# Retention and a bilinear FFN on one core: wide K^T V products with copied diagonal blocks in the opening, a later place for their totals, and the fifth group's outputs in one stretch

## The chip, the core and the metric

The kernel runs on one core of a Trainium2 chip. The engines of a core run their own queues of instructions, in order, and wait for each other by semaphores: TensorE (PE, matrix products into the PSUM banks, with PEld for the loads of its stationary operand), VectorE (DVE), ScalarE (ACT), GpSimd (POOL) and SyncE (SP, which issues most of the transfers). The metric is the device time of one execution in microseconds; lower is better. Three runs of the kernel before gave 324.79, 324.88 and 325.64 us, median 324.88.

## The reference

Inputs are `q`, `k`, `v` of shape (8 batches, 8 heads, 576 positions, 64), and three matrices of an FFN with 512 inputs, 1536 hidden units and 512 outputs. Everything is float32.

```python
scores = scale * np.matmul(q, k.transpose(0, 1, 3, 2))
Dmat = np.where(rel >= 0, gamma[:, None, None] ** rel[None, :, :], 0.0)
ret = scores * Dmat[None, :, :, :]
attn = np.matmul(ret, v)                  # (8, 8, 576, 64)
x = attn.transpose(0, 2, 1, 3).reshape(B * S, H * D)   # 4608 x 512
out = (x @ w_a) * (x @ w_b) @ w_out       # 4608 x 512
```

`rel` is the distance of a query from a key, and each head has its own `gamma` below 1. There is no softmax. So the attention can be computed in pieces: a block of queries needs its scores with the keys of its own block, and one 64 x 64 matrix per head, the sum of K^T V over all blocks before it (its "state"). The decay is put into the values (each row times a power of 1/gamma) and taken out again where the outputs are scaled.

## The kernel before

The 4608 tokens are worked on in FFN blocks of 512, 256, 256 and then seven of 512 tokens. A block makes, for each of twelve groups F of 128 hidden units, a product `pa` (x by w_a, line 869, or line 820 for the first two groups of the first block) and `pb` (x by w_b, line 884); ACT casts `pa` to `ha` (877), DVE multiplies `ha` by `pb` into `hT` (889), and twelve products `po` (831, 905) give 128 output rows, which ACT or DVE copies to `osb` and SP stores. The FFN is by far the larger part. The attention's work is put between its products.

The attention of the first 256 tokens of batches 0, 1 and 2 is done in six "steps", `STEPS` (line 165): step 0 is batch 0 with heads 0 to 3, step 1 batch 1 with heads 0 to 3, steps 2 and 3 the same batches with heads 4 to 7, steps 4 and 5 batch 2. A partition holds two neighbouring tokens, so partitions 0 to 63 are tokens 0 to 127 and partitions 64 to 127 the rest; `kp` is the token of a partition, `j` a pair of heads, `r` a head of the pair, and `half(i)` the lower or upper 64 partitions. Steps 0 to 3 make up the opening, before the first FFN product; steps 4 and 5 come later, between products of the first block. A step has these parts:

- `cast_step` (315) casts queries and keys to bfloat16 as `qkb`, `values_step` (318) multiplies the values by their decay into `vb`, each on an engine named in the call.
- `transpose_step` (329) turns `qkb` by four PE products for each of Q and K into a bank `tp`, and copies that to `qkT`.
- `score_step` (344) makes sixteen 64-column-wide score products into `sc`, which DVE masks into `sT` (360).
- `state_step` (366) makes K^T V by sixteen products of 64 x 64 (379): one tile `kvs[0]` for the first 128 tokens, one tile `kvs[1]` for the second 128. ACT copies the first into `state_after` (391), which the second half of the step's queries needs, and keeps both, as `own` (395) and `second` (396). `last_states` (403) does this for steps 1 and 3 together: 32 products, then two copies into `state_after` (412), one of `own` (414) and one of `second` (416).
- `open_step`, `step_states` (449) and `step_keys` (465) make the outputs, and `close_step` scales them on DVE into `xT` (486, 481), from which the FFN reads.
- `total_of(n)` (419), called later, adds `second` to `own` and casts the sum: the state after 256 tokens.

All other tokens are handled in "pairs" of 128-token pieces with all eight heads. Pairs 3, 4 and 5 are the second parts of batches 0, 1 and 2. For a pair, `keyed` makes K^T V, `matched` the scores and their mask, `open_outputs` (704) the products of the queries with the states (`from_states`, 668), and `close_outputs` (714) those of the scores with the values (`keys_into`, 681), into the same tile `o`; DVE then scales it in two operations (694). Between the two, `open_outputs` has ACT copy one column of `o` to a small tile named `fence` (711), so the instructions that follow and write that tile come after that copy.

The order on every engine is the order in which the program calls the parts. For the opening this is written out (lines 938 to 1015), with `warm` products (932) of a constant in between. From then on a list `todo` gives each piece of attention work a due count, in units of one 512-column product, and the work is issued at the next "edge" of the FFN's stream after that count: behind each `pb`, and behind every fourth product of the output stage. Small DVE and ACT pieces go into a list `later`, from which `pop` takes one at certain places, and `flush` all. Pair 5 (the "fifth group") is due as follows, in the third FFN block, where the edges of the output stage lie at 268, 272, 276, 280, 284 and 288:

```python
(252, stretch, (5, 4)), (274, open_alone, (5,)),
(278, close_outputs, (5,)), (336, stretch, (6, None)),
```

Of the kernel before, what the change touches and what calls it, by code (L numbers as in the profile page):

```python
# [10 lines left out]
FP32 = mybir.dt.float32  # L11
# [3 lines left out]
ALU = mybir.AluOpType  # L15
# [3 lines left out]
def kernel(  # L19
# [108 lines left out]
    def half(i):  # L128
        return slice(64 * i, 64 * i + 64)
# [99 lines left out]
    def pair_tables(step):  # L229
# [17 lines left out]
        else:  # L247
# [7 lines left out]
    second = sum_pool.tile([128, FIRST, HP, 64], FP32, tag="sums",  # L255
                           name="second")
# [58 lines left out]
    def cast_step(i, w, on):  # L315
        COPY[on](by_parity(natural[STEPS[i]][0][:, w]), given(i, w))  # L316
# [12 lines left out]
    def transpose_step(i, *ways):  # L329
        qkb, qkT = natural[STEPS[i]][0], transposed[STEPS[i]]  # L330
        tp = ps_ffn.tile([128, len(ways), 4, 128], BF16, tag="ab", name="tp")
        for to, (w, on) in enumerate(ways):
            for c in range(4):
                nc.tensor.transpose(tp[:, to, c, :],  # L334
                                    qkb[:, w, c * 128:c * 128 + 128],
                                    identity)
        for to, (w, on) in enumerate(ways):
            COPY[on](qkT[:, w], tp[:, to].rearrange("p c x -> p (c x)"))
# [5 lines left out]
    def score_step(i, place=None, tag="sc"):  # L344
        key = STEPS[i]
        sc = (place or ps_sc).tile([128, 2, 2, 2, 128], FP32, tag=tag,
                                   name="sc0")
        for j in (0, 1):
            for kp in (0, 1):
                for r, a in QUADS:  # L350
                    k0 = kp * 256 + j * 128 + a * 64
                    nc.tensor.matmul(  # L352
                        sc[half(a), r, j, kp],
                        transposed[key][half(r), 1, k0:k0 + 64],
                        queries(key, half(r), j, a),
                        start=(j == 0 and kp == 0), stop=True,
                        skip_group_check=True)
# [8 lines left out]
    def state_step(i, rest=None):  # L366
        state_copies(i, state_products(i, [
            ps_ffn.tile([128, 2, 64], FP32, tag="ab", name=f"kv0{a}")
            for a in (0, 1)], set(QUADS)), rest)

    def state_products(i, kvs, fresh):

        n, hh = STEPS[i]
        qkb, vb = natural[n, hh]
        for j in (0, 1):
            for kp in (0, 1):
                for a, r in QUADS:
                    e0 = kp * 256 + (2 * j + r) * 64
                    nc.tensor.matmul(kvs[a][half(r), j, :],
                                     qkb[half(a), 1, e0:e0 + 64],  # L380
                                     vb[half(a), e0:e0 + 64],
                                     start=(a, r) in fresh, stop=True,
                                     skip_group_check=True)
                    fresh.discard((a, r))
        return kvs

    def state_copies(i, kvs, rest=None):
        n, hh = STEPS[i]
        cs = slice(2 * hh, 2 * hh + 2)
        for r in (0, 1):  # L390
            nc.scalar.copy(state_after[half(r), n % 2, cs, half(r)],
                           kvs[0][half(r)])

        def keep():
            nc.scalar.copy(own_sums[n][:, cs], kvs[0])
            nc.scalar.copy(second[:, n, cs], kvs[1])

        if rest is None:
            keep()
        else:  # L400
            rest.append(keep)

    def last_states():

        own, later_half = kvs = [
            ps_ffn.tile([128, 2, 2, 64], FP32, tag="ab", name=f"kv1{a}")
            for a in (0, 1)]
        fresh = set(QUADS)
        for i in (1, 3):
            state_products(i, [kv[:, i // 2] for kv in kvs], fresh)  # L410
        for r in (0, 1):
            nc.scalar.copy(state_after[half(r), 1, :, half(r)],
                           own[half(r)].rearrange("p i j d -> p (i j) d"))
        nc.scalar.copy(own_sums[1],
                       own.rearrange("p i j d -> p (i j) d"))
        nc.scalar.copy(second[:, 1],
                       later_half.rearrange("p i j d -> p (i j) d"))

    def total_of(n):

        own = own_sums[n]
        if n < FIRST - 1:
            nc.gpsimd.tensor_tensor(own, own, second[:, n], op=ALU.add)
            nc.gpsimd.tensor_copy(own_states[n], own)
        else:
            nc.vector.tensor_tensor(own, own, second[:, n], op=ALU.add)
            nc.scalar.copy(own_states[n], own)
        sums_of[n, 0] = own

# [25 lines left out]
    def step_keys(i, fresh):  # L455

        n, hh = STEPS[i]
        vb = natural[n, hh][1]
        sT = scored.pop((n, hh))
        seen = set()  # L460
        for j in (0, 1):
            for kp in (0, 1):
                for a, r in QUADS:
                    e0 = kp * 256 + (2 * j + r) * 64
                    nc.tensor.matmul(  # L465
                        out_of(i, a)[half(r), 128 * j:128 * j + 128],
                        vb[half(a), e0:e0 + 64],
                        sT[half(a), r, j, kp],
                        start=(a in fresh and (a, r) not in seen), stop=True,
                        skip_group_check=True)  # L470
# [480 lines left out]
    warm(2, 512)  # L951
    score_step(0)
    warm(1, 512)
    state_step(0)
    transpose_step(2, (Q, "dve"))
    cast_step(2, K, "pool")
    cast_step(1, K, "pool")
    warm(2, 512)
# [14 lines left out]
    cast_step(3, K, "dve")  # L973
    score_step(1)
    cast_step(3, Q, "act")
    rest = []
    state_step(2, rest)
    warm(2, 512)
    transpose_step(3, (Q, "act"))
    transpose_step(3, (K, "dve"))  # L980
    rest.pop()()
    open_step(2)
    step_states(2, True)
    step_keys(2, {0})
# [2 lines left out]
    values_step(3, 0, nc.scalar)  # L987
    values_step(3, 1, pool_)
    load_w(*pieces[1], "b")
    score_step(3)  # L990
    close_step(2)
    last_states()
    for i, banks in ((1, ps_ffn), (3, ps_sc)):
        open_step(i, banks)
        step_keys(i, {0, 1})
    for i in (1, 3):
        step_states(i, False)
    for i in (1, 3):
# [4 lines left out]
    for c in (0, 1):  # L1003
        for F in range(WCOLS[0]):
            begin_with(F, c, 1)
    for piece in pieces[2:]:
        load_w(*piece)
    for i in (0, 1, 2):
# [56 lines left out]
    def third_turn():  # L1065
        for i in (4, 5):
# [83 lines left out]
```

## Time and profile before

| what | value |
|---|---|
| median of three runs | 324.88 us |
| profiled execution, its own time | 324.69 us |
| its span, first to last instruction | 322.9 us |
| PE busy | 313.5 us (97%), 3569 products recorded |
| DVE, ACT, POOL busy | 166.3, 130.8, 118.9 us |
| first product of the FFN (line 820) | 16.41 us from the start |
| first `pb` product (line 884) | 18.16 us |
| HBM | 37.75 MB read, 9.44 MB written |

A row of the timeline gives start and duration in us, the engine, the line, the operation, `out<-in` by the program's tile names, the form (for products `rows*columns` of the array first), and `xN` where N instructions in a row are shown as one; their duration is then that of all. In square brackets stands the idle time before and what ended it. A row of waits gives who waited for what: total, number of times, longest. A row by stretch gives its bounds, its length, and the busy time and count of PE, PEld, DVE, ACT and POOL, then the granted clock, the share of the transfer engines and GB/s. Durations of PE products include their way through the array, so one of 128 columns is shown with about 0.22 us though the next starts 0.06 us later.

### The profile page before, as it was taken

Reading aid. Unit: us, or ns where it says so; the run is one execution under the profiler, and the core shown is the slowest. Engines: PE = TensorE matmul, PEld = TensorE weight load, DVE = VectorE, ACT = ScalarE, POOL = GpSimd, SP = SyncE. Lnnn points to the kernel's source line nnn. Section 1 sums busy time; section 2 is a strip of 40 time slices with the busy share of each in tenths; the row PEclk is TensorE's granted clock in tenths of the full one; section 3 lists DMA queues with packets and bytes.
Section 4 is the critical chain, followed back from the end, with each engine's and each line's share of the span. In section 5 each row is a group of like instructions: output and inputs, shape, how many; then the busy total and the mean of one; then the engine's idle time right before and its main releaser. Section 6 shows DMA issues by size and latency. Waiting matters only on the chain.

```text
span 322.9 us, 8622 instructions
## 1 busy us (share of the span) xinstructions
PE 313.5 (97%) x3569; PEld 164.1 (51%) x3607; DVE 166.3 (51%) x296; ACT 130.8 (40%) x289; POOL 118.9 (37%) x159
## 2 busy tenths in 40 slices
PE   7899999999999999999999999999999999999996
PEld 3554457778444555454454545454445444444444
DVE  6745346667437664745374527461666256514411
ACT  7745653436335533523253324342433243313321
POOL 4990076574745365348174305550520000000000
DMA  8999999999999999899999169925840510031013
GB/s 216 253 204 207 263 227 197 193 176 207 197 213 234 201 193 229 214 223 262 209 208 194 67 146 199 215 67 146 202 78 28 135 37 2 2 97 32 1 25 107
DMA packets 146487, 50.90 MB, mean 158 GB/s; under 512 B 126736, under 2 KB 141968, under 8 KB 146448
## 3 DMA queue, kind: packets, MB, share of 16 engines
q1 hardware_dynamic: 140112, 45.37, 68.0%
q0 software_dynamic: 5808, 4.72, 9.3%
q8 instruction: 28, 0.46, 0.6%
q10 hardware_dynamic: 528, 0.26, 0.3%
q14 instruction: 11, 0.09, 0.1%
HBM read 37.75 MB, written 9.44 MB: 146 GB/s over the span
## 4 chain that ended last, share of the span: by engine, by line
PE 93%; DMA 2%; POOL 1%; issue 1%; SPq 1%; DVE 0%; POOLq 0%
PE pb L884 29%; PE pa L869 28%; PE po L905 27%; DMA vf<-in_v_dram 2%; PE po L831 2%; PE o L681 1%; PE sc L640 1%; PE o L668 1%; PE kv L573 1%; SPq L159 1%; POOL vb L326 1%; PE pa L820 1%; PE o L465 0%; PE tp L334 0%; POOL wb_sb L266 0%
## 5 line engine op out<-in xcount | busy, mean ns | idle before, releaser
L889 DVE TENSOR_TENSOR hT<-ha,pb 128x512 bf16<-128x512 bf16 (+1 forms) x120 | 75.9, 633 | 91.3 <-PE pb L884 83.3
L884 PE MATMUL pb<-xT,wb_sb 128*128 128x512 bf16 (+1 forms) x473 | 111.3, 358 | 0.5
L877 ACT CAST ha<-pa 128x512 bf16<-128x512 f32 (+1 forms) x120 | 64.8, 542 | 112.8 <-PE pa L869 108.2
L869 PE MATMUL pa<-xT,wa_sb 128*128 128x512 bf16 (+1 forms) x457 | 108.1, 357 | 1.1 <-issue 0.6
L905 PE MATMUL po<-wo_sb,hT 128*128 128x512 bf16 (+2 forms) x419 | 89.6, 367 | 1.6 <-issue 1.4
L884 PEld LDWEIGHTS <-wb_sb 128*128 128x128 bf16 x480 | 47.0, 98 | 46.2
L869 PEld LDWEIGHTS <-wa_sb 128*128 128x128 bf16 x472 | 45.4, 98 | 44.6
L905 PEld LDWEIGHTS <-hT 128*128 128x128 bf16 x432 | 40.4, 98 | 44.4
L519 POOL CAST qkb<-qf 64x1024 bf16<-64x1024 f32 x15 | 15.4, 1030 | 67.0 <-DMA qf<-in_q_dram 61.3
L530 POOL TENSOR_TENSOR vb<-vf,vs 128x1024 bf16<-128x1024 f32 (+1 forms) x17 | 28.8, 1699 | 12.7 <-DMA vf<-in_v_dram 7.5
L916 DVE COPY osb<-po 128x512 f32<-128x512 f32 (+2 forms) x16 | 10.4, 650 | 38.9 <-PE po L905 38.9
L914 ACT COPY osb<-po 128x512 f32<-128x512 f32 (+1 forms) x20 | 11.4, 572 | 46.2 <-PE po L905 43.3
L519 POOL CAST qkb<-kf 64x1024 bf16<-64x1024 f32 (+1 forms) x17 | 15.9, 933 | 14.8 <-DMA kf<-in_k_dram 14.4
L598 DVE TENSOR_TENSOR sums<-kv,sums 128x256 f32<-128x256 f32 x44 | 18.7, 424 | 2.8 <-PE kv L573 0.8
L649 DVE TENSOR_TENSOR sT<-sc,mask 128x512 bf16<-128x512 f32 x30 | 19.5, 682 | 0.0
L523 POOL CAST qkb<-kf 64x512 bf16<-64x512 f32 (+1 forms) x34 | 18.6, 575 | 1.0
L523 POOL CAST qkb<-qf 64x512 bf16<-64x512 f32 x30 | 17.6, 614 | 0.6
L694 DVE TENSOR_TENSOR xT<-o,qs 128x512 bf16<-128x512 f32 x24 | 15.5, 682 | 2.6 <-PE o L681 2.6
L601 ACT CAST states<-sums 64x512 bf16<-64x512 f32 x26 | 16.0, 617 | 0.3
L316 POOL CAST qkb<-kf 128x512 bf16<-128x512 f32 x4 | 2.4, 612 | 16.1 <-DMA kf<-in_k_dram 16.1
L360 DVE TENSOR_TENSOR sT<-sc,mask_s 128x1024 bf16<-128x1024 f32 x6 | 7.3, 1224 | 1.5 <-PE sc L352 1.3
L932 PE MATMUL w<-ones 128*128 128x512 bf16 x17 | 6.3, 483 | 1.5 <-DVE idxp_f L204 1.5
(96 smaller groups left out, 173.0 us busy)
## 6 DMA issues: line engine op xcount, KB each, us to landing
qf<-in_q_dram SPq DMA_DIRECT2D x32, 256.0 KB, 4.7
vf<-in_v_dram SPq DMA_DIRECT2D x32, 256.0 KB, 5.0
kf<-in_k_dram SPq DMA_DIRECT2D x31, 256.0 KB, 4.7
out_dram<-osb SPq DMA_DIRECT2D x25, 256.0 KB, 2.4
out_dram<-osb SPq DMA_DIRECT2D x21, 128.0 KB, 2.8
wo_sb<-in_moe_w_out_dram POOLq DMA_DIRECT2D x3, 512.0 KB, 16.2
qf<-in_q_dram SPq DMA_DIRECT2D x8, 128.0 KB, 3.3
kf<-in_k_dram SPq DMA_DIRECT2D x8, 128.0 KB, 3.5
```

Of the source, the lines that this page charges most:

```text
L519: nc.gpsimd.tensor_copy(qkb[0:64, w, e], t[0:64, e])
L523: nc.gpsimd.tensor_copy(to[:, :, 1 - r], fro[:, :, r])
L530: nc.gpsimd.tensor_tensor(vb[:, e].rearrange("p (h d) -> p h d", d=D), t[:, e].rearrange("p (h d) -> p h d", d=D), decay[:, at], op=ALU.mult)
L598: nc.vector.tensor_tensor(sums[:, i], own, prev, op=ALU.add)
L601: return [lambda r=r: nc.scalar.copy(to(half(1 - r)), fro(half(r))) for r in (0, 1)]
L649: nc.vector.tensor_tensor(sT[:, on].rearrange("p c k s -> p (c k) s"), sc[:, on].rearrange("p c k s -> p (c k) s"), mask3.unsqueeze(1).to_ ...
L694: nc.vector.tensor_tensor(x_of(t0, 128).rearrange("p c (a s) -> p c a s", a=2), o[:, :, :, kp].rearrange("p a c s -> p c a s"), qs[:, :, s ...
L869: nc.tensor.matmul(pa[:, 0:n], wa_sb[:, c, fs], xT[:, c], start=(c == 0), stop=(c == NC - 1))
L877: nc.scalar.copy(ha[:, 0:n], pa[:, 0:n])
L884: nc.tensor.matmul(pb[:, 0:n], wb_sb[:, c, fs], xT[:, c], start=(c == 0), stop=(c == NC - 1))
L889: nc.vector.tensor_tensor(hT[:, F, 0:n], has[F][:, 0:n], pb[:, 0:n], op=ALU.mult)
L905: nc.tensor.matmul(po[:, 0:width], hT[:, F, u * 128:(u + 1) * 128], wo_sb[:, F, cols], start=(F == 0), stop=(F == NF - 1))
```

## The change

Four things are changed in the opening, and one later.

1. K^T V of steps 0 to 3 is made by 128-column products (two heads by two heads), of which only the two diagonal 64 x 64 blocks are used (`diagonal`). `wide_products` on the lower 64 partitions gives the state after the first 128 tokens, copied block by block into `state_after` (`own_copies`); on all 128 partitions it gives the state after 256 tokens, copied block by block into `own_sums` (`total_steps`). So `second` is only left for steps 4 and 5, and `total_of` adds nothing for batches 0 and 1.
2. The two warm products behind step 2's K^T V are gone, and step 3's keys are turned before its queries.
3. `close_step(2)` stands before `score_step(3)`. The wide products of steps 1 and 3 stand each before the key products of that step.
4. The totals of steps 1 and 3 (eight products, two copies) stand behind the first twelve products of line 820, instead of before the state products.
5. `close_outputs(5)` is due at 274.1 instead of 278, the same edge as `open_alone(5)`.

```diff
+    def diagonal(t, r):
+        return t[half(r), :, half(r)]
+
+    def wide_products(steps, rows, kv=None, fresh=True):
+        if kv is None:
+            kv = ps_ffn.tile([128, len(steps), 2, 128], FP32, tag="ab", name="kvw")
+        for at, i in enumerate(steps):
+            qkb, vb = natural[STEPS[i]]
+            for j in (0, 1):
+                for kp in (0, 1):
+                    e0 = kp * 256 + j * 128
+                    nc.tensor.matmul(kv[:, at, j, :],
+                                     qkb[rows, K, e0:e0 + 128],
+                                     vb[rows, e0:e0 + 128],
+                                     start=(fresh and at == j == kp == 0),
+                                     stop=True, skip_group_check=True)
+        return kv.rearrange("p i j d -> p (i j) d")
+
+    def own_copies(steps, kv):
+        n, cs = heads_of(steps)
+        for r in (0, 1):
+            nc.scalar.copy(state_after[half(r), n % 2, cs, half(r)],
+                           diagonal(kv, r))
+
+    def own_step(i):
+        own_copies([i], wide_products([i], half(0)))
+
+    def total_steps(*steps):
+        kv = wide_products(steps, slice(0, 128))
+        n, cs = heads_of(steps)
+        def keep():
+            for r in (0, 1):
+                nc.scalar.copy(own_sums[n][half(r), cs], diagonal(kv, r))
+        return keep
...
         if n < FIRST - 1:
-            nc.gpsimd.tensor_tensor(own, own, second[:, n], op=ALU.add)
             nc.gpsimd.tensor_copy(own_states[n], own)
...
-    state_step(0)
+    own_step(0)
+    keep = total_steps(0)
     transpose_step(2, (Q, "dve"))
+    keep()
...
-    rest = []
-    state_step(2, rest)
-    warm(2, 512)
+    own_step(2)
+    keep = total_steps(2)
+    transpose_step(3, (K, "dve"))
     transpose_step(3, (Q, "act"))
-    transpose_step(3, (K, "dve"))
-    rest.pop()()
+    keep()
...
+    close_step(2)
     score_step(3)
-    close_step(2)
-    last_states()
-    for i, banks in ((1, ps_ffn), (3, ps_sc)):
+    own = ps_ffn.tile([128, 2, 2, 128], FP32, tag="ab", name="kv13")
+    for at, (i, banks) in enumerate(((1, ps_ffn), (3, ps_sc))):
+        wide_products([i], half(0), own[:, at:at + 1], at == 0)
         open_step(i, banks)
         step_keys(i, {0, 1})
+    own_copies([1, 3], own.rearrange("p i j d -> p (i j) d"))
...
     for c in (0, 1):
         for F in range(WCOLS[0]):
             begin_with(F, c, 1)
+    total_steps(1, 3)()
...
-             (278, close_outputs, (5,)), (336, stretch, (6, None)),
+             (274.1, close_outputs, (5,)), (336, stretch, (6, None)),
```

More of the change, by code (lines that the diff above doesn't have):

```diff
@@ L254 @@
                 for n in range(FIRST)]
-    second = sum_pool.tile([128, FIRST, HP, 64], FP32, tag="sums",
-                           name="second")
+    second = sum_pool.tile([128, HP, 64], FP32, tag="sums", name="second")
     own_states = [const.tile([128, HP, 64], BF16, name=f"first{n}")
@@ L364, in score_step, with heads_of @@
             .to_broadcast([128, 4, 256]), op=ALU.mult)
[L366 to L369, printed above, removed]
+    def diagonal(t, r):
+        return t[half(r), :, half(r)]
+    def wide_products(steps, rows, kv=None, fresh=True):
+        if kv is None:
+            kv = ps_ffn.tile([128, len(steps), 2, 128], FP32, tag="ab",
+                             name="kvw")
+        for at, i in enumerate(steps):
[9 more added lines that the diff above has]
+        return kv.rearrange("p i j d -> p (i j) d")
+    def heads_of(steps):
+        n, hh = STEPS[steps[0]]
+        return n, slice(2 * hh, 2 * hh + 2 * len(steps))
+    def own_copies(steps, kv):
[12 more added lines that the diff above has]
+        return keep
     def state_products(i, kvs, fresh):
@@ L395, in keep @@
             nc.scalar.copy(own_sums[n][:, cs], kvs[0])
-            nc.scalar.copy(second[:, n, cs], kvs[1])
+            nc.scalar.copy(second[:, cs], kvs[1])
         if rest is None:
@@ L401, in state_copies @@
             rest.append(keep)
[L403 to L417, printed above, removed]
     def total_of(n):
@@ L422, in total_of @@
         if n < FIRST - 1:
-            nc.gpsimd.tensor_tensor(own, own, second[:, n], op=ALU.add)
             nc.gpsimd.tensor_copy(own_states[n], own)
         else:
-            nc.vector.tensor_tensor(own, own, second[:, n], op=ALU.add)
+            nc.vector.tensor_tensor(own, own, second, op=ALU.add)
             nc.scalar.copy(own_states[n], own)
```

## The prediction

> **What bounds the kernel now.** Read first the page (span, chain of what ended last), then the busy time by stretch, then the timeline of the opening and of the stretch around 83 us.
>
> ```profile
> span 322.9 us, 8622 instructions
> PE 93%; DMA 2%; POOL 1%; issue 1%; SPq 1%; DVE 0%; POOLq 0%
> 18.00:60.00 42.00, 41.63 (x397) 24.35 (x401) 19.96 (x37) 21.53 (x54) 21.37 (x37) 1.00 1.22 219
> PE po L905 <- issue: 1.4, 9, 0.2
> ```
>
> The chain is TensorE (PE) for 93%; from 18 us on PE is busy 41.63 of 42.00 us, and its waits after 18.2 us name no engine. So whatever PE work is added after 18 us, and whatever delays the first FFN product, reaches the end in full; nothing later absorbs it. The opening is different: it waits for inputs and other engines. Its last part, ACT first, then PE:
>
> ```profile
> 12.02 0.62 ACT L316 CAST qkb<-qf 128x512 bf16<-128x512 f32 x1 [0.22 <-DMA qf<-in_q_dram]
> 12.54 0.53 ACT L391 CAST state_after<-kv 64x128 bf16<-64x128 f32 x2
> 13.12 0.59 ACT L338 COPY qkT<-tp 128x512 bf16<-128x512 bf16 x1
> 13.61 0.27 ACT L395 COPY own<-kv 128x128 f32<-128x128 f32 x1
> 13.76 0.28 ACT L396 COPY second<-kv 128x128 f32<-128x128 f32 x1
> 13.92 1.07 ACT L324 ACTIVATE vb<-vf,vs 128x64 bf16<-128x64 f32 x4
> 15.33 0.74 ACT L412 CAST state_after<-kv 64x256 bf16<-64x256 f32 x2 [0.34 <-PE kv L379]
> ...
> 9.49 0.40 PE L334 MATMUL tp<-identity,qkb 128*128 128x128 bf16 x4
> 12.69 0.62 PE L334 MATMUL tp<-identity,qkb 128*128 128x128 bf16 x8 [0.24 <-ACT qkb L316]
> 15.70 0.55 PE L465 MATMUL o<-sT,vb 64*64 64x128 bf16 x25 [0.29 <-issue]
> 16.18 0.40 PE L449 MATMUL o<-qkT,state_after 128*128 128x128 bf16 x4
> 16.41 1.91 PE L820 MATMUL pa<-xT,wa_sb 128*128 128x256 bf16 x16
> ```
>
> To see: ACT never rests from 12.02 to 14.99; its multiplications (13.92) make the values of step 3, without which the last K^T V products cannot be made, nor the state copies (15.33 to 16.07), nor the state products at 16.18. From there PE runs on into the FFN. And the fifth group's outputs:
>
> ```profile
> 82.82 0.58 ACT L914 COPY osb<-po 128x512 f32<-128x512 f32 x1 [0.66 <-PE po L905]
> 83.31 0.17 ACT L711 COPY fence<-o 128x2 f32<-128x2 f32 x1
> 82.94 0.22 PE L668 MATMUL o<-qkT,states 64*64 64x64 bf16 x5
> 83.09 1.04 PE L905 MATMUL po<-wo_sb,hT 128*128 128x512 bf16 x4
> 84.06 0.45 PE L681 MATMUL o<-sT,vb 64*64 64x64 bf16 x32
> ...
> 76.81 0.16 ACT L711 COPY fence<-o 128x2 f32<-128x2 f32 x1 [0.76 <-PE o L668]
> 77.02 0.45 PE L681 MATMUL o<-sT,vb 64*64 64x64 bf16 x32
> 77.40 0.61 PE L869 MATMUL pa<-xT,wa_sb 128*128 128x256 bf16 x4
> ```
>
> To see: the key products (L681) write the bank that the small ACT copy "fence" reads, so they come after it: it ended at 76.97 and they began at 77.02. At 83 us four FFN products lie between and hide the fence, which stands behind the 0.58 us output copy on ACT.
>
> **Part 1, steps 0 and 2: wide products.** Sixteen 64-column products (0.32 us a step) become four on 64 rows and four on 128 rows. Eight 128-column products: the rows for 4 and 8 transposes differ by 0.22 us for four, 0.056 each, so 0.45. Step 0: the start is held by ACT's values at 6.84, so 6.89 + 0.45 = 7.34, and the next transposes waited for POOL until 7.39 anyway: nothing. Step 2: from 11.59 to 12.04; the two warm products (11.84 to 12.45) go, K's transposes (cast done 11.83) come first and Q's wait for ACT's cast at 12.64 as before: nothing. With these covers gone a step would cost the 0.13 us between 0.32 and 0.45. Q's copy on ACT stays at 13.12, since the two state copies before it end at 13.07. DVE's copy of K moves from 13.35 to 13.04 (its mask ends then); the scores of step 3, which waited for it until 13.83, now wait for Q's copy (13.71 + 0.05 = 13.77).
>
> **Part 2, close of step 2 ahead of the last scores.** On DVE the scaling (0.68) goes from 13.80 to 14.48; behind it stands the mask of step 3 (1.23), which begins at 14.40 instead of 14.30 and ends at 15.63 instead of 15.52. The key products of step 3 wait for that: 15.68 + 0.25, done well before the states below: nothing, or 0.10 if ACT were not later still. Behind the mask the scalings of steps 1 and 3 start when the state products end, as now.
>
> **Part 3, ACT's kept copies.** Two copies of 128 partitions (13.61, 13.76), each overlapping the one before by 0.1, so 0.21 from the end of Q's copy (13.71) to 13.92, become two of 64 partitions from strided blocks. The nearest row is L391: two take 0.53, one 0.26, so no overlap. Bounds: as cheap as now, 0; overlapped at both outer ends, 13.61 + 0.53 - 0.10 = 14.04, +0.12; at none, 13.71 + 0.53 + 0.03 = 14.27, +0.35. I take the middle of the last two, +0.24, as L391 is the like form. Queued behind on ACT are the four multiplications, hence the K^T V products, hence the state copies: 15.33 + 0.24, and 0.03 because one more wide product follows the last value than now: 15.60 + 0.74 = 16.34; PE 0.055 later (cast over 12.64, transposes 12.69) at 16.40, for 16.18: **+0.22**. Now, PE is held there not by ACT (16.07 + 0.05 = 16.13) but by 25 key products that began only at 15.70, after an "issue" gap. That gap goes or falls into the FFN's backlog, but ACT is late next. Bounds: -0.03 with copies as cheap as now, +0.34, and 0.10 more if the 64-row products cannot hide their weight loads (0.10 each).
>
> **Part 4, totals of steps 1 and 3 moved among the FFN products.** Of 32 products before the states, eight wide ones remain; eight come after twelve of the sixteen first FFN products. PE has no gap there, for step 3's scaling is done by 17.8 and the last four products come at about 18.0. So eight times 0.056, **+0.45**. Bounds: 0 if a gap opens there; 0.78 if each load (98 ns in the FFN rows) lies bare. I keep the transposes' row: same shape. Two copies on ACT (0.37 each) move from 16.1 to about 18.8, ahead of the two FFN casts, which so end near 20.1 and 20.6; the first hT was due at 19.30 against a bank that PE needs back only at 22: nothing. The move issues no DMA, so SP's and POOL's queues keep their order; POOL loses two adds (0.73 each at 22.5 and 23.7) that nobody waited for.
>
> The Trainium skill's page "TensorE: Matmul & The Clock Gate", section "Back-to-back issue gap", gives about 81 ns for a 128-column product in a stream of loads and products; the trace's transposes, also one load each, show 56. By the page the eight cost 0.65 and the sum below would be 1.20, 326.1.
>
> **Part 5, the fifth group.** Now: states from 82.72, four products from 83.09, keys 84.06, and (keys to FFN 0.38, as 77.02 to 77.40) FFN again at 84.44. Less the four products (4 x 0.216 = 0.86) that is 83.58. After: both run at the same edge, states then keys; the fence still starts at 83.31 behind the output copy, ends 83.48, keys at 83.53, FFN at 83.91: **+0.33**. The whole FFN is queued behind this wait on PE, and nobody else is ready to use the time. If nothing held the keys they would follow the last states at 82.99, FFN at 83.37: -0.21, the saved switch between shapes. Upper end +0.40, ACT a little later. The two DVE scalings (1.29) move forward into idle time (2.60 before them): nothing.
>
> **Sum.** 0.22 + 0.45 + 0.33 = 1.00. The profiled execution took 324.69 (span 322.9 and 1.8 around it), so 325.69; the median of three is 324.88, 0.19 above, so **325.9**, 0.31% slower. What a measurement here can tell from no change is about 0.3%, 0.97 us: the forecast lies just past it.
>
> **Rivals.**
> - *The fence does not hold the keys* (not slower). If the ACT wait is over when the last states end, part 5 gives -0.21: 0.46 in all, **325.3**. For: the wait hidden today shows no cost. Against: 76.81/77.02, where the keys start 0.05 after the fence although scores ran between. It decides as soon as the keys start before 83.5. Chance 0.13.
> - *Bare weight loads.* Parts 3 and 4 at their upper ends: 0.44 + 0.78 + 0.33 = 1.55, **326.4**. For: all products of a block use the same rows, and 64-row by 128-column ones are nowhere in the trace. Against: the transposes. Chance 0.13.
> - *PE falls to half speed* after the warm products go. Row: five 512-column products took 2.10 us at 2.78 (0.42 each), two took 0.59 at 5.54 (0.22), though the granted clock reads 1.00 throughout. Half speed for 3.4 us, as long as the start had, costs 1.7 more: **327.6**. Against: the eight extra wide products replace 0.43 us of warm work. Chance 0.04. The same page, "What's actually happening", has a fall only after an idle window of about 3.4 us; gaps here stay under 0.6, so by that rule, too, none.
> - *The moved totals fill a gap and ACT's copies cost nothing*: -0.03 + 0 + 0.33 = 0.30, **325.2**. Chance 0.10.
> - *Faster by over 0.3%*: all low ends together are -0.24; no row gives more. 0.05 for what I do not see.
>
> **Numbers.** The forecast case holds 0.55 of the chance; with its terms uncertain by some 0.3, I put 0.41 of this past 0.97 and 0.14 below. Slower: 0.41 + 0.13 + 0.04 = 0.58; within: 0.14 + 0.13 + 0.10 = 0.37; faster: 0.05. The range, 325.1 to 326.6, leaves out the half clock and the unseen gain and takes in the two cheaper cases and the bare loads.
>
> **What would show it.** State products of steps 1 and 3 near 16.4 (now 16.18) with ACT's L324 row starting near 14.16; eight wide products of about 0.45 us in front of the last first-layer products and the first pb near 18.83 (now 18.16); the fence ending 0.05 before the fifth group's keys, with PE idle about 0.5 between states and keys. Wrong if ACT's half copies overlap, if the keys start at once, or if a matmul row lasts twice as long after 13 us.

## The result, and the profile after

The changed kernel takes 328.00 us (median; 327.63 to 328.37) beside 324.88 for the kernel before (324.65 to 325.64): a ratio of 1.0098, with a 95% interval of 1.0087 to 1.0109. The forecast was 325.9, at most 326.6. It is slower, as forecast, but by 3.1 us instead of 1.0. The profiled execution took 328.2 us, 3.5 more than the one before. The page of the changed kernel:

```profile
span 326.5 us, 8588 instructions
PE 92%; DMA 2%; SPq 2%; ACT 1%; DVE 1%; issue 1%
```

The span has grown by 3.6 us, and PE still carries the chain. Where PE lost the time is best seen by following the same products in both traces and noting how much later each starts than before. The difference is constant for long stretches and grows in four places:

| place | product | before | after | later by | grown by |
|---|---|---|---|---|---|
| opening | first `pb` | 18.16 | 18.90 | 0.74 | 0.74 |
| first block | a `pb` product in the 52nd us | 51.58 | 53.18 | 1.60 | 0.86 |
| second block | a key product of a later pair | 77.19 | 80.33 | 3.14 | 1.54 |
| fifth group | the output product that stood first behind its keys before | 84.45 | 87.89 | 3.44 | 0.30 |
| end | span | 322.9 | 326.5 | 3.6 | 0.16 |

The first and the fourth were in the forecast (0.67 and 0.33). The second and the third, 2.4 us together, were not. The last 0.16 comes in several steps, which I did not follow. PE's longest waits in the changed kernel (who waited for what: total, number, longest):

```profile
PE o L701 <- issue: 1.3, 1, 1.3
PE pb L904 <- DVE osb L936: 0.7, 1, 0.7
PE o L701 <- ACT fence L731: 0.4, 1, 0.4
```

Three single waits, each of them once, hold most of what was added behind the opening. They are taken here in order of time.

**The opening.** The timeline of the changed kernel, ACT's rows and PE's:

```profile
13.70 0.53 ACT L405 COPY own<-kvw 64x128 f32<-64x128 f32 x2
14.26 1.06 ACT L323 ACTIVATE vb<-vf,vs 128x64 bf16<-128x64 f32 x4
15.68 0.74 ACT L393 CAST state_after<-kv 64x256 bf16<-64x256 f32 x2 [0.36 <-PE kv L379]
16.48 0.40 PE L469 MATMUL o<-qkT,state_after 128*128 128x128 bf16 x4 [0.21 <-ACT state_after L393]
18.02 0.61 PE L379 MATMUL kvw<-vb,qkb 128*128 128x128 bf16 x8
18.90 0.38 PE L904 MATMUL pb<-xT,wb_sb 128*128 128x512 bf16 x1
```

To see: the two kept copies take 0.53, no overlap, and the values begin at 14.26 (forecast 14.16, before 13.92); the state products begin at 16.48 (forecast 16.40), and PE waits there for ACT's copies; eight totals stand among the first FFN products; the first `pb` comes at 18.90 (forecast 18.83). In this execution ACT's copies of step 2 began 0.09 later already (the cast of step 3's queries, ahead of them on ACT, waited for its input until 12.11 instead of 12.02), which accounts for the rest.

**At 52 us.** First the kernel before, the addition of `own` and `second` of batch 2 on DVE and the multiplication on POOL that follows:

```profile
49.86 0.46 DVE L426 TENSOR_TENSOR own<-own,second 128x256 f32<-128x256 f32 x1
51.30 1.90 POOL L530 TENSOR_TENSOR vb<-vf,vs 128x1024 bf16<-128x1024 f32 x1 [1.26 <-ACT ha L877]
```

Then the changed kernel:

```profile
50.34 1.90 POOL L550 TENSOR_TENSOR vb<-vf,vs 128x1024 bf16<-128x1024 f32 x1
50.60 1.93 DVE L446 TENSOR_TENSOR own<-own,second 128x256 f32<-128x256 f32 x1
52.45 0.68 DVE L936 COPY osb<-po 128x512 f32<-128x512 f32 x1
53.18 0.60 PE L904 MATMUL pb<-xT,wb_sb 128*128 128x256 bf16 x4 [0.69 <-DVE osb L936]
```

To see: before, the addition ended 0.98 us before POOL's multiplication began. DVE has moved 0.74 later with PE, and the multiplication has come 0.96 earlier, and now the addition begins inside it. DVE's shift alone would not have done this: an addition from 50.60 to 51.06 is still clear of a multiplication at 51.30. The multiplication waits for two transfers of values; the second was issued at 45.0 us before and 45.1 after, and landed at 50.7 and 50.1. In the nine profiles of the changed kernel and its variants that leave the start of the opening as it is, the multiplication begins between 50.1 and 50.5; in the two such profiles of the kernel before, at 50.73 and 51.30. Why it comes earlier is not shown. The addition takes 1.93 us instead of 0.46. Behind it on DVE stands the copy of an output bank, and PE needs that bank: the wait.

**At 79 us.** PE's rows in a stretch of attention products; and below them, from the view of the transfers, the queue of PE's own instructions between 77.5 and 79.0 us (number of transfers, MB, share of the engines):

```profile
78.62 0.38 PE L701 MATMUL o<-sT,vb 64*64 64x64 bf16 x24
80.33 0.26 PE L701 MATMUL o<-sT,vb 64*64 64x64 bf16 x8 [1.33 <-issue]
```

```profile
q8 instruction: 1, 0.02, 5.4%
```

To see: of 32 key products 24 run, then PE stands for 1.5 us from start to start, with its operands there and no engine named ("issue"), then the last eight run. The stretch is 128 short products, each with its own load: 256 rows of PE's instructions in about 1.2 us of work. Just as it begins, at 77.62, a transfer of 16 KB of instructions starts; it takes 1.30 us, and PE goes on 2.71 after its start.

**At 86 us**, ACT's fence and PE's keys of the fifth group:

```profile
86.42 0.17 ACT L731 COPY fence<-o 128x2 f32<-128x2 f32 x1
86.64 0.44 PE L701 MATMUL o<-sT,vb 64*64 64x64 bf16 x32 [0.36 <-ACT fence L731]
```

To see: the fence ends at 86.59 and the keys start 0.05 later, 0.55 after the start of the last state product (86.09): as forecast.

### The profile page after: what moved, and what is told of

Its sections match the earlier page's. It is cut to its first block, busy times and chain, and to the rows that moved or that the text cites. A ratio compares the mean times of both kernels' runs of the same rounds, so it can differ in the third digit from the quotient of the medians.

```text
span 326.5 us, 8588 instructions
## 1 busy us (share of the span) xinstructions
PE 318.6 (98%) x3573; PEld 165.2 (51%) x3573; DVE 166.7 (51%) x296; ACT 131.0 (40%) x289; POOL 117.7 (36%) x157
## 4 chain that ended last, share of the span: by engine, by line
PE 92%; DMA 2%; SPq 2%; ACT 1%; DVE 1%; issue 1%
PE pb L904 29%; PE pa L889 28%; PE po L925 27%; DMA qf<-in_q_dram 2%; SPq L159 2%; PE po L851 2%; PE o L701 2%; PE sc L660 1%; PE o L688 1%; PE kv L593 1%; PE pa L840 1%; DVE own L446 0%; PE tp L333 0%; DVE xT L506 0%; ACT vb L323 0%
## 5 line engine op out<-in xcount | busy, mean ns | idle before, releaser
L889 PE MATMUL pa<-xT,wa_sb 128*128 128x512 bf16 (+1 forms) x472 | 109.8, 358 | 0.0
L925 PE MATMUL po<-wo_sb,hT 128*128 128x512 bf16 (+2 forms) x432 | 91.6, 367 | 0.0
L539 POOL CAST qkb<-kf 64x1024 bf16<-64x1024 f32 (+1 forms) x17 | 16.1, 950 | 18.3 <-DMA kf<-in_k_dram 17.8
L701 PE MATMUL o<-sT,vb 64*64 64x64 bf16 x480 | 7.2, 195 | 1.7 <-issue 1.3
## 6 DMA issues: line engine op xcount, KB each, us to landing
wo_sb<-in_moe_w_out_dram POOLq DMA_DIRECT2D x3, 512.0 KB, 16.1
```

The lines of the kernel that those rows point to most:

```text
L539: nc.gpsimd.tensor_copy(qkb[0:64, w, e], t[0:64, e])
L889: nc.tensor.matmul(pa[:, 0:n], wa_sb[:, c, fs], xT[:, c], start=(c == 0), stop=(c == NC - 1))
L925: nc.tensor.matmul(po[:, 0:width], hT[:, F, u * 128:(u + 1) * 128], wo_sb[:, F, cols], start=(F == 0), stop=(F == NF - 1))
```

## The experiments

The theory after this reading: (a) the opening costs 0.7, by the steps that the prediction named; (b) the shift of DVE and POOL against each other makes the addition meet the multiplication, 0.86; (c) the change has 68 rows fewer on PE, a row being a weight load or a product of PE's program (7146 for 7214; the expectations count two more in every kernel), so the fetched blocks of instructions fall elsewhere, and one block now lies almost wholly in a stretch that PE works off faster than the next can be fetched, 1.5; (d) the fence, 0.33. The rival for (b) and (c): they belong to the changed code itself, the new shape of `second` or the changed products. Each kernel ran beside the kernel before on the same chip, so ratios are the thing to compare.

**Padding at the start.** PE's count of rows is restored by short products that nobody reads.

```diff
-    warm(8, 512)
+    warm(5, 512, 37)      # and 37 products of 64x64x64
```

> The changed kernel with 34 more PE products in the opening: three of the eight first warm products are replaced by 37 short ones of 64 x 64, in the same 3.4 us in which PE waits for inputs. All later PE instructions keep their order but stand 68 places further back in PE's stream, where they stood in the kernel before. Theory (the 1.5 us hole in the key products at 78.81 to 80.33 is PE waiting for its next 16 KB block of instructions): the hole goes, the time falls by 1.4 to 1.6 us to about 326.5; the long DVE add at 50.6 stays. Rival (the hole belongs to the new order of the work, whatever the place in the stream): hole and time stay, 328.0.

Measured: 327.70 (326.54 to 329.51), ratio 1.0076 [1.0048, 1.0104]. The hole at 79 us is gone. But something else came: granted clock (the last column but two) in this kernel from 17.65 us on; it was 1.00 up to there:

```profile
17.65:21.00 3.35, 3.35 (x22) 2.62 (x21) 0.94 (x2) 0.03 (x1) 3.35 (x6) 0.50 1.18 167
```

To see: from 17.64 to 21.05 TensorE ran at half clock, and PE's lag to the kernel before grew there from 1.06 to 3.0. That is the prediction's third rival, in a kernel which took away three of the eight products of the start. Three of its six executions kept the full clock (326.54, 326.60 and 327.62). The row count stands as a cause; the price can't be read here.

**The three costs undone one by one and together, with this padding.** The addition later, out of POOL's multiplication:

```diff
-    todo += [(136, total_of, (2,))]
+    todo += [(166, total_of, (2,))]
```

> The changed kernel with total_of(2), the DVE add of own and second and the cast behind it, due at a count of 166 instead of 136, when GpSimd is between two pieces of work. Theory (the add took 1.93 us instead of 0.46 because GpSimd's multiplication of 50.34 to 52.24 ran at the same time): the add takes 0.4 to 0.5 us again, the output copy behind it is not late, PE's 0.86 us gap at 52.2 goes, and the time falls by 0.7 to 0.9 us to about 327.2. Rival (the add is slow because second is now a smaller tile in another place): the add still takes 1.9 us, wherever it stands, and the time falls by at most what its new neighbours leave uncovered.

Measured: 327.31 (326.52 to 327.56), ratio 1.0060 [1.0044, 1.0077]. The addition takes 0.60 us at 57.20, beside short casts on POOL, PE's wait at 52 us is gone; the hole (1.3) and the fence's wait are still there. Against 1.0098 this gives back some 0.0038, 1.2 us, uncertain by about 0.6 by the two intervals: theory (b), 0.86, is inside.

```diff
-             (274.1, close_outputs, (5,)), (336, stretch, (6, None)),
+             (278, close_outputs, (5,)), (336, stretch, (6, None)),
```

> The changed kernel with the fifth group's key products due at 278 again, four products behind its state products. Theory (as predicted, the fence holds them when nothing lies between): the 0.53 us wait between states and keys goes, two switches of 0.09 come back, and the time falls by 0.3 us to about 327.7. Rival (one stretch is worth its saved switches and the 3.1 us come from elsewhere alone): the time rises by 0.2 us.

Measured: 327.64 (327.31 to 328.04), ratio 1.0077 [1.0061, 1.0094]. In the trace four output products stand between the last states and the keys again, the keys follow without a wait, and PE's lag does not grow there (3.1 before and after). Theory (d) stands by the trace; the time itself, 0.36 under 328.00, is about as small as such runs can tell apart.

> All three at once: the 34 short products, the add at 166, the fifth group's outputs apart. What is left of the change is the opening. Theory (the causes are separate and add up): 328.0 - 1.5 - 0.85 - 0.3 = 325.3 to 325.7, that is 0.5 to 0.8 us above the kernel before, the opening's own cost. Rival (the late start of the FFN costs more by other collisions further on): 326 or more.

Measured: 327.57 (326.05 to 327.70), ratio 1.0062 [1.0042, 1.0082]. Behind 21 us PE's lag stays between 3.0 and 3.1 to the end: no wait for the addition, no hole, no fence. But in the profiled execution the clock was halved from 17.18 to 20.60, as above; the two executions with the full clock took 326.05 and 326.32, still over the expectation: with the padding at the start the FFN begins 1.04 us later than before already, instead of 0.3. So the padding had to stand where it does not touch the start.

**The padding in a wait.** Now 34 short products stand where PE waits for ACT's state copies anyway (16.1 to 16.5):

```diff
+    short(34)
     own_copies([1, 3], own.rearrange("p i j d -> p (i j) d"))
```

> The changed kernel with 34 short products (64x64x64 on halves of the tile of ones, into a tile that nobody reads) placed on PE just before ACT's copies of the states of steps 1 and 3, where PE waits for ACT anyway. They are 68 more rows on PE, so that its rows have the numbers again that they had before the change (7216 in all). Theory (the 1.5 us hole in the fifth stretch is a fetch of PE's instructions, whose place goes by the count of rows): the hole goes, the addition that meets POOL's multiplication stays at 1.7 to 1.9 us, the fence keeps its 0.3; 328.0 - 1.5 = 326.5. The products take 34 x 0.03 = 1.0 us at most of a wait of 0.5, so up to 0.5 of it can come back: 326.5 to 327.0. Rival (the hole comes from what stands in the stretch, keys and outputs, not from the count): it stays at 78 us, and the time is 328.0 to 328.5. If the half clock of the padded runs before came from PE's early products that were taken away there, the granted clock stays 1.0 here.

Measured: 326.75 (326.46 to 327.62), ratio 1.0048 [1.0031, 1.0065], with the full clock. The 32 key products run as one row at 78.44. The state products begin at 17.12, more than the wait could cover, so some of the gain is given back. In the profiled execution the addition began later in POOL's multiplication, took 1.11 us, and PE did not wait for it.

**A small dose.** Eight short products (16 rows) in the same place.

> The same with 8 short products in place of 34: 16 rows, 7164 in all. Theory: PE reaches the block that has to be fetched 16 short rows later in the stretch, and those rows cover a part of the wait, 16 x 0.055 = 0.9 us; the hole is 0.5 to 0.8 instead of 1.3 to 1.5, and the time 327.1 to 327.4. Rival (the count of rows doesn't matter): 1.3 to 1.6 and 328.0.

Measured: 326.65 (325.81 to 327.47), ratio 1.0039 [1.0020, 1.0058]; the profiled execution took 327.26. Its rows in the stretch:

```profile
78.79 0.32 PE L701 MATMUL o<-sT,vb 64*64 64x64 bf16 x16
79.38 0.32 PE L701 MATMUL o<-sT,vb 64*64 64x64 bf16 x16 [0.27 <-issue]
```

To see: with 16 rows more ahead, PE stops 8 products (16 rows) earlier in the stretch, at the same count of rows, and the hole is 0.46 instead of 1.5. A cause in the code of the stretch would not move with rows put in 60 us earlier. Why the median is lower than I expected, and no higher than with all 34, is not shown: the executions go from 325.81 to 327.47, and the trace is of one of the slowest.

**All three undone, with the padding in the wait.**

> The 34 short products in PE's wait, the sum of own and second of group 2 at count 166 instead of 136, and the fifth group's outputs at 278 again. Theory: of the 3.1 us that the change costs, the hole (1.5), the addition (0.86) and the fence (0.33) are gone, and the opening's 0.7 is left: 325.4 to 325.9. Rival (the three holes only move and come back elsewhere, or the padding itself costs): 326.5 or more.

Measured: 325.87 (325.72 to 326.41), ratio 1.0018 [1.0000, 1.0035]. In the trace PE's lag is 1.08 at the first `pb` (0.35 of it from the padding) and stays between 1.0 and 1.2 to the end. So the four places are the whole of it: what is left is the opening, with its padding.

**The collision in the kernel before.** Nothing is changed there but the due count of the addition.

```diff
-    todo += [(136, total_of, (2,))]
+    todo += [(146, total_of, (2,))]
```

> The kernel before, with nothing changed but the sum of own and second of group 2 asked for at count 146 instead of 136, some 1.5 us later, so that DVE's addition, which reads two tiles of SBUF, falls into POOL's multiplication at 51.3 to 53.2. Theory (the two slow each other down): the addition takes 1 to 2 us instead of 0.46, the copy of the outputs behind it on DVE is late, PE waits 0.3 to 0.9 for it: 325.2 to 325.8. Rival (the addition was long in the changed kernel for a reason of that kernel, the new shape of second): 0.46 us still, and 324.9.

Measured: 326.28 (325.26 to 328.12), ratio 1.0031 [1.0010, 1.0053].

```profile
50.73 1.90 POOL L530 TENSOR_TENSOR vb<-vf,vs 128x1024 bf16<-128x1024 f32 x1 [0.49 <-PE po L905]
51.85 1.06 DVE L426 TENSOR_TENSOR own<-own,second 128x256 f32<-128x256 f32 x1
...
53.73 0.60 PE L869 MATMUL pa<-xT,wa_sb 128*128 128x256 bf16 x4 [0.56 <-ACT ha L877]
```

To see: the same operation, of the old shape, takes 1.06 us as soon as it starts inside POOL's multiplication, and PE waits 0.56 (for a cast of ACT that stood behind). So the rival falls. The profiled execution took 325.32; most took about 326.3, half a microsecond over the expectation, for which I have no trace. (The longest, 328.12, ran at a mean clock of 0.995.)

The five profiles in which the addition starts inside the multiplication show how: it ends 0.28 us after the multiplication does, whenever it began.

| kernel | multiplication | addition | ends after it by |
|---|---|---|---|
| changed | 50.344 to 52.244 | 50.600 to 52.525 | 0.281 |
| outputs apart | 50.181 to 52.081 | 50.583 to 52.360 | 0.279 |
| eight short products | 50.458 to 52.360 | 50.586 to 52.641 | 0.281 |
| 34 short products | 50.167 to 52.067 | 51.241 to 52.347 | 0.280 |
| kernel before, addition later | 50.727 to 52.628 | 51.849 to 52.909 | 0.281 |

Whether the two overlapped for 0.8 or for 1.8 us, the same 0.28 is left when the multiplication ends, so the addition makes no headway while it runs; the multiplication keeps its 1.90 us. (Alone the addition takes 0.46; why 0.28 is enough behind the multiplication is not shown.) The Trainium skill's page "SBUF — State Buffer", section "SBUF: two separate sides", says that a VectorE operation with two SBUF inputs and a GpSimd operation that reads SBUF lock each other out for a whole instruction, the one that starts first holding the ports that they share; the trace agrees in all five. VectorE's products of `ha` by `pb`, one of whose inputs is in PSUM, take 0.42 us in both kernels, beside POOL or not.

**The hole in the kernel before.** 94 short products make 188 more rows; 188 and -68 differ by 256. All the attention code is that of the kernel before.

```diff
-    warm(2, 512)                # ahead of the weights' first load
+    warm(2, 512, 50)
...
-    warm(2, 512)                # behind step 2's K^T V
+    warm(2, 512, 32)
...
+    todo += [(9, warm, (0, 0, 12))]
-    todo += [(136, total_of, (2,))]
+    todo += [(166, total_of, (2,))]
```

> The kernel before with 94 short products (64x64x64, read by nobody): 82 of them behind warm products of the opening where PE waits 0.8 and 0.6 us, 12 in the first feed-forward block, and the sum of own and second at count 166, out of POOL's way. Its PE rows are 7404, 188 more than before; 188 and -68 (the change's) differ by 256, the rows of one fetched block, so the fifth stretch lies on the block boundaries as in the changed kernel. Theory (the hole is set by where the rows fall on blocks of 256): a hole of 1.3 to 1.6 us opens in the fifth stretch's key products at 78 to 81 us, in a kernel that has nothing of the change, and the time is 1.5 more, plus 0.2 to 0.5 for the products that the waits don't cover: 326.6 to 327.0. Rival (the hole belongs to the changed code): no hole, 325.2 to 325.6.

Measured: 328.13 (327.74 to 329.51), ratio 1.0102 [1.0085, 1.0120]. PE's rows in the opening and in the fifth stretch:

```profile
15.32 0.19 PE L935 MATMUL w<-ones 64*64 64x64 bf16 x1 [1.49 <-issue]
...
80.54 0.38 PE L681 MATMUL o<-sT,vb 64*64 64x64 bf16 x23
82.04 0.26 PE L681 MATMUL o<-sT,vb 64*64 64x64 bf16 x9 [1.12 <-issue]
```

To see: the hole opens in the unchanged stretch, after 23 of the 32 key products, 1.3 us from start to start. And there is a second one that I had not reckoned with, which is why the time is 1.1 to 1.5 over the expectation: the 32 short products in the opening stop before the last, for 1.7 us. Counted in PE's instructions as the program lists them, from 0 and with the semaphore waits between the rows, the product behind the stop has number 450 here, and number 2242 in the stretch; in the changed kernel it has 1987, and in the one with eight short products too. 2242 is 450 plus seven times 256, and 1987 is 450 plus six times 256 and one: always the same boundary. And 450 is also the product behind the "issue" gap at 15.70 us in the kernel before. (The clock was halved for 3.4 us in the profiled execution, 329.51, and full in the others.)

**The totals in the wait.** As with all undone, but the eight totals of steps 1 and 3 come out of the FFN products into PE's wait, with 20 short products instead of 34.

```diff
+    keep = total_steps(1, 3)
+    short(20)
     own_copies([1, 3], own.rearrange("p i j d -> p (i j) d"))
     for i in (1, 3):
         step_states(i, False)
+    keep()
...
-    total_steps(1, 3)()
```

> The kernel with all three costs undone (padding in PE's wait, sum at 166, outputs at 278), and the eight total products of steps 1 and 3 taken from among the first feed-forward products into PE's wait for ACT's state copies, in place of 14 of the 34 short ones (7188 rows). Theory (part 4 of the prediction: each of the eight costs 0.056 on the path): the first pb comes 0.45 earlier than with all three undone, at 18.8 instead of 19.24, and the time is 325.87 - 0.45 = 325.4. Rival (the eight fill a time in which PE has slack, or their place costs as much in the wait): 325.8 to 326.0.

Measured: 325.60 (325.49 to 326.15), ratio 1.0021 [1.0012, 1.0030].

```profile
17.37 1.91 PE L840 MATMUL pa<-xT,wa_sb 128*128 128x256 bf16 x16
19.12 1.24 PE L904 MATMUL pb<-xT,wb_sb 128*128 128x512 bf16 x5
```

To see: from the first `pa` to the first `pb` it is 1.75 us now; with the totals in between it was 2.19 (17.05 to 19.24). The difference, 0.45, is eight times 0.056, so part 4's price is right to the hundredth. But my filling was longer than the wait, the states came 0.33 later, and of the gain 0.12 is left at the first `pb`: no difference that the ratios can show.

**A version meant to beat both.** The sum at 166, the outputs at 278, step 2's kept copies behind the values of step 3, the totals ahead of step 3's keys, and each total product cut into two of 64 columns, which adds the rows without adding columns.

```diff
-                    nc.tensor.matmul(kv[:, at, j, :],
+                    for c in range(cut):      # cut=2 for the totals
+                        wd = 128 // cut
+                        nc.tensor.matmul(kv[:, at, j, wd * c:wd * c + wd],
                                          qkb[rows, K, e0:e0 + 128],
-                                     vb[rows, e0:e0 + 128],
+                                         vb[rows, e0 + wd * c:e0 + wd * c + wd],
...
-    keep()
     open_step(2)
...
     values_step(3, 0, nc.scalar)
+    keep2()
...
+        if i == 3:
+            own_copies([1, 3], own.rearrange("p i j d -> p (i j) d"))
+            keep = total_steps(1, 3)
+            keep()
         step_keys(i, {0, 1})
```

> A version meant to beat both: the changed kernel, with the sum at 166 and the outputs at 278; ACT's kept copies of step 2 behind the values of step 3 instead of ahead (part 3); the eight totals of steps 1 and 3 ahead of step 3's key products, where PE waits for DVE's scores, their copies right behind the state copies; and each total product cut into two of 64 columns, 32 more rows (7180), so that the blocks of 256 rows fall otherwise and no hole opens in the fifth stretch. Theory: part 3's 0.25 and part 4's 0.45 go, the first pb comes at 18.2 to 18.5, and the time is 324.9 to 325.3. Rival (64-column products take as long as 128-column ones, or ACT's copies of the totals hold PE): 325.4 to 326.

Measured: 324.87 (324.55 to 325.19) beside 324.89 for the kernel before, ratio 0.9995 [0.9985, 1.0004]. The first `pb` comes at 18.43, 0.47 earlier than in the changed kernel and 0.27 later than before; the stretch at 77 us has no hole, the fence and the addition cost nothing. The whole loss is recovered; nothing is gained.

> The same, and the scores of step 3 ahead of the outputs of step 2 again, as in the kernel before (part 2, which the prediction priced at nothing). Theory of the prediction (part 2 is free): the same time as with the scores later, within 0.15. Rival (step 3's key products wait for DVE, which now does the outputs' sum of 0.69 us first): with the scores first the key products of step 3 begin 0.35 earlier, the first pb comes at 17.9 to 18.2, and the time is 324.6 to 324.9, under the kernel before.

Measured: 325.00 (324.77 to 327.89), ratio 1.0010 [0.9994, 1.0027]; first `pb` at 18.43. The order of step 2's outputs and step 3's scores makes no difference, as part 2 had it. The test is a mild one: the totals keep PE busy there until the scores are masked in either order.

## Why the prediction was wrong

- **Parts 1 and 2, nothing.** Held. Nothing of steps 0 and 2 shows up in PE's lag, and the order of scores and outputs gave the same first `pb` both ways.
- **Part 3, +0.22, and part 4, +0.45.** Held: 0.74 at the first `pb`, 0.09 of it from inputs that came later in that execution, so 0.65 for 0.67. ACT's half copies take 0.53 for two, without overlap, the value taken. The eight totals measured 0.45.
- **Part 5, +0.33.** Held: 0.30, the keys 0.05 behind the fence. The rival that the fence would not hold them fell.
- **The step that failed is the sum**, with the sentence it rests on: that what delays the first FFN product "reaches the end in full; nothing later absorbs it". Nothing absorbed it, but I took this to mean that a shift arrives unchanged. A shift of 0.74 us moves PE, ACT and DVE against POOL, which waits for transfers and whose multiplication moved too, 0.96 the other way. The trace of before had the two rows, an addition ending at 50.32 and a multiplication on the next engine starting at 51.30; that DVE stands still while the second runs is not seen there, but a term, or a rival, "an operation on DVE meets one on POOL" was missing. It cost 0.86. Part 4's sentence that POOL's queue keeps its order was right; its times did not stay.
- **The second miss, in part 1 and part 4: rows that go were priced by the time they take alone.** Half as many products of double width, and fewer warm ones, leave PE 68 rows shorter, and that moved a block boundary into the densest stretch, 60 us later: 1.54. The profile of before shows the transfers (28 on PE's instruction queue) and an "issue" gap of 0.5 at 15.2 us; I read the gap as a thing of its place and never asked what fetches PE's instructions.
- **The half clock**, rival three, 1.7 us at 0.04. It is real (1.9 us in the padded kernel) but did not come into the changed one's five executions. It is no property of the change: one of the 35 executions of the kernel before that ran beside the padding in the wait took 327.97 at a mean clock of 0.995, and that mean is what 3.41 us at half clock give over 326 us. What decides it stays open.
- **The bare weight loads** fell: the wide products of 128 rows run 0.056 apart, and so do those of 64 rows where nothing else holds them (four in 0.39 us at 15.20 in the last version but one, the final 0.22 of it the way through the array).

With the two terms put in, the sum is 0.65 + 0.30 + 0.86 + 1.54 = 3.35 of the 3.6 us; inputs and small steps are the rest.

## What to carry to other kernels

A change of the opening is not only a shift: list the places where an engine paced by transfers meets one paced by PE, and ask for each what happens when they come a microsecond or two closer, since both can move (here 0.74 and 0.96). Two operations that keep clear of each other by chance, as here by one microsecond, are best kept apart by their due times; a later due count cost nothing. And count instructions too, not only time: where a stretch of 256 rows of PE lasts under the 2.5 to 2.8 us measured here from a transfer's start to the next product, any edit ahead of it that adds or removes rows can open or close a hole (0.5 to 1.7 us here), so a small difference between two versions should be looked at in that place first.

## What the runs showed of the hardware

- PE's instructions come in transfers of 16 KB, 256 instructions each: 28 for the 7241 of the kernel before, 29 for the 7429 of the one with 94 short products, and the stops lie a multiple of 256 apart. In eight holes PE went on 2.5 to 2.8 us after the start of the transfer: 13.16 to 15.70 in the kernel before; 77.62 to 80.33 in the changed one; 77.08 to 79.61 with the addition later; 77.45 to 80.28 with the outputs apart; 76.81 to 79.38 with eight short products; 13.20 to 15.81 in the kernel before with the addition later; 12.79 to 15.32 and 79.25 to 82.04 in the kernel before with 94. For the block in question the transfer started just after PE had entered the block ahead: at row 1728 (71.42 us) in the kernel before, with 80 rows of the FFN still to come before the stretch, and at row 1752 in the changed one, when the stretch had begun. Other transfers in these traces started up to 3 us before or 4 us after PE entered the block ahead; what sets this is not shown. A block that PE works off in less time than that shows the fetch. The Trainium skill's page "Runtime: NRT & Kernel Launch", section "Instruction fetch mechanics", has the blocks of 256 and calls the cost of crossing one mostly hidden. The size agrees; here one crossing cost 1.5 us, and the measurement decides.
- An addition on DVE of two SBUF tiles stands still while a multiplication on POOL runs, and ends 0.28 us after it (five profiles, table above).
- The granted clock can fall to half for 3.41 us in the opening without PE having rested that long: in three profiles (padding at the start, with and without the other edits, and the 94 products) it did, each time 10.24 us, three times 3.41, after the clock had first been full; PE's longest wait in the 3.41 us ahead was between 0.5 and 1.5 us, and its waits there were 0.9 to 1.5 us in all. By the mean clock (0.990 or 0.995) some executions without a profile had it too: two of the kernel with the padding at the start, three of the one with all three costs undone and this padding, and one each of the kernel before, of the kernel before with the addition later and of the last version. The Trainium skill's page "TensorE: Matmul & The Clock Gate", section "What's actually happening", which the prediction used to rule it out, names an idle window of that length; what these windows had of idleness was a part only.
